# Layer 0's activation chain by one feature tile instead of two

## The chip, the cores and the metric

The kernel runs on one core of a Trainium2 chip. The metric is the device time of one execution in microseconds (us); lower is better. Beside it the profiler leaves a trace of one execution, from which all rows below are taken.

## The reference

Three results are computed in one launch: an attention with a window of 128 and 4 sink tokens, and two dense layers one after the other on 1536 tokens. Cut to what matters here:

```
h = x @ w_in                                   # 1536x512 @ 512x2048
sp = np.where(h > 20.0, h, np.log1p(np.exp(np.minimum(h, 20.0))))
g = h * np.tanh(sp)                            # layer 0's activation
y = g @ w_out                                  # 1536x2048 @ 2048x512
...
g = h * np.clip(h + 3.0, 0.0, 6.0) / 6.0       # layer 1's, on y with its own weights
```

## The kernel before

**Work and stages.** Attention comes first, layer 0 next and layer 1 last, but they overlap. The attention of the first eight 128-token blocks is done alone; the remaining blocks' attention is cut into pieces that are issued from within layer 0's steps. All weights arrive as 64-bit words and are decoded on VectorE (DVE) and ScalarE (ACT): two mask and shift operations (L210, L211), one that joins them (L212), a float16 high part on ACT (L222) and the float16 rest on DVE (L224). Layer 1's weights take a check (L215 on ACT), their own splits (L249, L250) and some sums (L260 to L268). Every product is three float16 matmuls: high by high, high by low, low by high.

**A step of layer 0.** There are 24. A step has `up` (L728) and `down` (L766). `up` multiplies two feature tiles of 128 features by 512 tokens; each tile has 12 matmuls (L745 to L747) and its own PSUM bank `h`, out of the four of the pool `ps_h`. Then comes the activation chain: Exp out of PSUM (L748, ACT), Square (L753, ACT), Ln (L754, ACT), Exp (L755, ACT), the product with `h` (L757, DVE, which is the last reader of the bank), the float16 high half `gh` (L761, ACT) and the low half `gl` (L762, DVE). L748 and L757 go over one tile at a time, the other five over both tiles, 1024 elements per partition. `down` multiplies the result `g16` by the second weights (L790, 24 matmuls), adding to four banks of the pool `ps_acc`. It lags by one step, so TensorE (PE) sees up(s), down(s-1), up(s+1), down(s). Layer 1 has the same form (L814 to L832 up, L854 down, L875 the sums that free its accumulators).

**What shares the banks.** The attention's scores `s` (L349, L556; read by L353 and L563 on DVE) and its output `o` take banks of the same pool `ps_h` in turn.

**What sets the order.** `hook()` is called after each tile of `up` and twice in `down`. It issues the next pieces of attention and of the decode; the decode pieces have a lower priority. A scheduler then fixes for each engine one static queue, in which an instruction that waits holds up all behind it. Raw weights have two buffers, so a load starts when the decode two before is done.

Of the kernel before, what the change touches and what calls it, by code (L numbers as in the profile page):

```python
# [8 lines left out]
F16 = mybir.dt.float16  # L9
I32 = mybir.dt.int32  # L10
I16 = mybir.dt.int16
AF = mybir.ActivationFunctionType
ALU = mybir.AluOpType
# [8 lines left out]
SX = 12  # L22
SW = 12
SG = 12
# [5 lines left out]
def attention_moe_moe2(  # L30
# [13 lines left out]
    nc = tc.nc  # L44
# [21 lines left out]
    g_p = main.enter_context(tc.tile_pool(name="g", bufs=LAG + 1))  # L66
# [16 lines left out]
    one = const.tile([128, 1], F32)  # L83
    fifth = const.tile([128, 1], F32)
# [17 lines left out]
    def watch(ap):  # L102
        i = n_low[0]
        n_low[0] += 1
        sq = const.tile([128, 64], F32, tag="sq", name="sq")
        nc.vector.tensor_tensor_reduce(out=sq, in0=ap, in1=ap, scale=1.0, scalar=0.0, op0=ALU.mult, op1=ALU.max, accum_out=lows[:, i:i + 1])
# [620 lines left out]
    def per_bank(blk):  # L727
        return 512 // (len(blocks[blk]) * 128)  # L728

    def up(st):  # L730
        layer, blk, f = st
        T = len(blocks[blk]) * 128
        per = per_bank(blk)
        x = xt[blk]
        e = e_p.tile([128, 2, per * T], F32, tag="e", name="e")
        hps = []
        for i in range(2):
            hp = ps_h.tile([128, per * T], F32, tag="h", name="h")
            for m in range(per):
                w = wt[layer, 0, f + i * per + m]  # L740
                o = hp[:, m * T:(m + 1) * T]
                for c in range(KD):
                    wh = w[:, 0, c * 128:(c + 1) * 128]
                    wl = w[:, 1, c * 128:(c + 1) * 128]
                    nc.tensor.matmul(o, wh, x[:, 0, c, :], start=c == 0, stop=False)  # L745
                    nc.tensor.matmul(o, wh, x[:, 1, c, :], start=False, stop=False)  # L746
                    nc.tensor.matmul(o, wl, x[:, 0, c, :], start=False, stop=c == KD - 1)  # L747
            nc.scalar.activation(out=e[:, i], in_=hp, func=AF.Exp, scale=2.0 ** -(SW + SX))  # L748
            hps.append(hp)
            hook()  # L750


        nc.scalar.activation(out=e, in_=e, func=AF.Square, bias=one)  # L753
        nc.scalar.activation(out=e, in_=e, func=AF.Ln, bias=fifth, scale=0.2)  # L754
        nc.scalar.activation(out=e, in_=e, func=AF.Exp, scale=-1.0)  # L755
        for i in range(2):
            nc.vector.scalar_tensor_tensor(out=e[:, i], in0=e[:, i], scalar=2.5, in1=hps[i], op0=ALU.subtract, op1=ALU.mult)  # L757
        sc = -0.4 * 2.0 ** (SG - SW - SX)
        g16 = g_p.tile([128, 2, 2 * per, T], F16, tag="g16", name="g16")
        gh, gl = (g16[:, i].rearrange("p (a b) n -> p a (b n)", a=2) for i in range(2))  # L760
        nc.scalar.activation(out=gh, in_=e, func=AF.Copy, scale=sc)  # L761
        nc.vector.scalar_tensor_tensor(out=gl, in0=e, scalar=sc, in1=gh, op0=ALU.mult, op1=ALU.subtract)  # L762
        gt[st] = g16
        if blk == 0 and f == 0:
            watch(g16[:, 0, 0, 0:64])
# [180 lines left out]
    def hook():  # L946

        if "at1" in late:
            budget["credit"] += budget["att"] / 4
        while budget["credit"] >= 1:  # L950
            att_side.piece()
            budget["credit"] -= 1
        for _ in range(DPS):
            if dec_side.n < budget["lim"]:
                with tc.high_priority(offset=-DEC_BACK):
                    dec_side.piece()
        if budget["chk"]:
            chk_side.piece()
# [273 lines left out]
```

## Time and profile before

| what | value |
|---|---|
| median of 3 runs | 595.24 us (595.04 to 595.64) |
| the profiled execution | 595.09 us, of which the trace spans 593.3 us |
| PE busy | 576.4 us, 97% |
| DVE busy | 461.7 us, 78% |
| ACT busy | 401.3 us, 68% |

The profiled execution lies 0.15 us below the median, and 1.8 us of it lie outside the span. Busy shares are means over stages that differ much; the stage has to be looked at for each wait.

### The profile page before, as it was taken

Reading aid. Unit: us, or ns where it says so; the run is one execution under the profiler, and the core shown is the slowest. Engines: PE = TensorE matmul, PEld = TensorE weight load, DVE = VectorE, ACT = ScalarE, POOL = GpSimd, SP = SyncE. Lnnn points to the kernel's source line nnn. Section 1 sums busy time; section 2 is a strip of 40 time slices with the busy share of each in tenths; the row PEclk is TensorE's granted clock in tenths of the full one; section 3 lists DMA queues with packets and bytes.
Section 4 is the critical chain, followed back from the end, with each engine's and each line's share of the span. In section 5 each row is a group of like instructions: output and inputs, shape, how many; then the busy total and the mean of one; then the engine's idle time right before and its main releaser. Section 6 shows DMA issues by size and latency. Waiting matters only on the chain.

```text
span 593.3 us, 11399 instructions
## 1 busy us (share of the span) xinstructions
PE 576.4 (97%) x4426; PEld 393.8 (66%) x4426; DVE 461.7 (78%) x1106; ACT 401.3 (68%) x794; POOL 22.4 (4%) x40
## 2 busy tenths in 40 slices
PE   8999999999999999999999999999999999999996
PEld 4787754444545445544444468888888888888885
DVE  5789999599944347489998999976687889864754
ACT  5998787699787578678978886544354656553532
POOL 0141010400000000000000000000000000000000
PEclk9999999999999999999999999999999999999999
DMA  9976357999762122252545442200017676400001
GB/s 176 244 166 200 114 172 165 211 259 249 200 141 31 26 39 57 39 160 82 173 141 173 142 143 72 72 1 2 1 30 250 217 261 216 148 21 1 36 1 39
DMA packets 105842, 72.24 MB, mean 122 GB/s; under 512 B 73512, under 2 KB 98088, under 8 KB 105784
## 3 DMA queue, kind: packets, MB, share of 16 engines
q1 hardware_dynamic: 105784, 71.48, 43.7%
q8 instruction: 35, 0.57, 0.4%
q14 instruction: 23, 0.19, 0.1%
HBM read 60.43 MB, written 3.15 MB: 107 GB/s over the span
## 4 chain that ended last, share of the span: by engine, by line
PE 65%; DVE 18%; ACT 9%; issue 3%; DMA 3%; SPq 1%; POOL 0%; DVEq 0%; ACTq 0%; POOLq 0%
PE acc L854 17%; PE acc L790 10%; PE h L816 6%; PE h L814 6%; PE h L815 6%; PE h L745 4%; PE h L747 4%; PE h L746 3%; PE s L349 2%; PE o L390 2%; DVE p L212 2%; DVE e L757 2%; DVE w L268 2%; DVE g L762 2%; ACT e L753 1%
## 5 line engine op out<-in xcount | busy, mean ns | idle before, releaser
L790 PE MATMUL acc<-g,w 128*128 128x512 f16 x576 | 130.1, 379 | 2.1 <-DVE g L762 1.7
L854 PE MATMUL acc<-w,g 128*128 128x256 f16 x1008 | 114.0, 273 | 0.2 <-DVE ob L875 0.2
L854 PEld LDWEIGHTS <-g 128*128 128x128 f16 x1008 | 98.6, 98 | 11.8 <-issue 0.4
L815 PE MATMUL h<-xt,w 128*128 128x256 f16 x384 | 104.7, 273 | 0.0
L816 PE MATMUL h<-xt,w 128*128 128x256 f16 x384 | 104.7, 273 | 0.0
L814 PE MATMUL h<-xt,w 128*128 128x256 f16 x384 | 104.7, 273 | 0.0
L790 PEld LDWEIGHTS <-w 128*128 128x128 f16 x576 | 55.3, 98 | 68.2 <-issue 3.4
L745 PE MATMUL h<-xt,w 128*128 128x512 f16 x192 | 72.8, 379 | 3.8 <-DVE e L757 3.6
L747 PE MATMUL h<-xt,w 128*128 128x512 f16 x192 | 72.8, 379 | 0.0
L746 PE MATMUL h<-xt,w 128*128 128x512 f16 x192 | 72.8, 379 | 0.0
L818 ACT ACTIVATE e<-h,bias 128x512 f32<-128x512 f32 x48 | 32.5, 678 | 47.7 <-PE h L816 47.6
L819 DVE SCALAR_TENSOR_TENSOR e<-e,h 128x512 f32<-128x512 f32 x48 | 32.7, 682 | 38.0 <-ACT e L818 38.0
L831 ACT ACTIVATE g<-e 128x256 f16<-128x256 f32 x96 | 29.5, 354 | 30.1 <-DVE e L819 30.1
L831 ACT ACTIVATE g<-sm 128x512 f16<-128x512 f32 x48 | 30.2, 628 | 27.3 <-DVE sm L826 27.2
L757 DVE SCALAR_TENSOR_TENSOR e<-e,h 128x512 f32<-128x512 f32 x48 | 30.8, 683 | 19.6 <-ACT e L755 19.5
L748 ACT ACTIVATE e<-h 128x512 f32<-128x512 f32 x48 | 28.2, 588 | 18.6 <-PE h L747 18.6
L832 DVE SCALAR_TENSOR_TENSOR g<-sm,g 128x512 f16<-128x512 f32 x48 | 33.0, 687 | 10.0 <-ACT g L831 9.9
L815 PEld LDWEIGHTS <-w 128*128 128x128 f16 x384 | 37.6, 98 | 4.5
L814 PEld LDWEIGHTS <-w 128*128 128x128 f16 x384 | 37.6, 98 | 4.5
L816 PEld LDWEIGHTS <-w 128*128 128x128 f16 x384 | 37.6, 98 | 4.4
L212 DVE SCALAR_TENSOR_TENSOR p<-raw,y 128x1024 int32<-128x1024 int32 x32 | 39.4, 1232 | 0.4
L746 PEld LDWEIGHTS <-w 128*128 128x128 f16 x192 | 18.8, 98 | 24.6 <-issue 3.6
(176 smaller groups left out, 949.4 us busy)
## 6 DMA issues: line engine op xcount, KB each, us to landing
raw<-in_moe_w_in_dram SPq DMA_DIRECT2D x48, 512.0 KB, 4.1
raw<-in_moe_w_out_dram SPq DMA_DIRECT2D x48, 512.0 KB, 5.1
out_dram<-ob SPq DMA_DIRECT2D x12, 256.0 KB, 2.6
first<-in_k_dram SPq DMA_DIRECT2D x8, 256.0 KB, 4.6
first<-in_q_dram SPq DMA_DIRECT2D x8, 256.0 KB, 5.0
first<-in_v_dram SPq DMA_DIRECT2D x8, 256.0 KB, 4.7
nk<-in_k_dram SPq DMA_DIRECT2D x5, 256.0 KB, 3.2
nv<-in_v_dram SPq DMA_DIRECT2D x5, 256.0 KB, 3.1
```

The costliest lines, as they stand in the source:

```text
L212: nc.vector.scalar_tensor_tensor(out=p, in0=t[:, :, 1], scalar=3, in1=y, op0=ALU.logical_shift_left, op1=ALU.bitwise_xor)
L745: nc.tensor.matmul(o, wh, x[:, 0, c, :], start=c == 0, stop=False)
L746: nc.tensor.matmul(o, wh, x[:, 1, c, :], start=False, stop=False)
L747: nc.tensor.matmul(o, wl, x[:, 0, c, :], start=False, stop=c == KD - 1)
L757: nc.vector.scalar_tensor_tensor(out=e[:, i], in0=e[:, i], scalar=2.5, in1=hps[i], op0=ALU.subtract, op1=ALU.mult)
L790: nc.tensor.matmul(o, l_, r_, start=first and m == 0 and x == 0, stop=last and end and x == 2, skip_group_check=True)
L814: nc.tensor.matmul(o, wh, x[:, 0, c, :], start=c == 0, stop=False)
L815: nc.tensor.matmul(o, wh, x[:, 1, c, :], start=False, stop=False)
L816: nc.tensor.matmul(o, wl, x[:, 0, c, :], start=False, stop=c == KD - 1)
L831: nc.scalar.activation(out=g[:, 0, d_], in_=src, func=AF.Copy, scale=sc)
L832: nc.vector.scalar_tensor_tensor(out=g[:, 1, d_], in0=src, scalar=sc, in1=g[:, 0, d_], op0=ALU.mult, op1=ALU.subtract)
L854: nc.tensor.matmul(a[n // 2][:, n % 2], l_, r_, start=f == fa and m == 0 and n % 2 == 0 and x == 0, stop=ends and m == 1 and x == 2 and (n ...
```

## The change

After a tile's matmuls, all seven operations of its chain are issued for that tile alone, each on 512 elements per partition, and then `hook()` is called. Before, `hook()` stood right behind the first Exp of a tile, and the rest of the chain behind both tiles. The tile `g16` is now allocated at the start of `up`, and its layout in memory is unchanged. In the changed file the chain stands at L749 to L756: first Exp L749, Square L750, Ln L751, second Exp L752, product L753, `gh` L755, `gl` L756; later lines are five less than before (L790 is L785, L875 is L870).

```
-        hps = []
+        g16 = g_p.tile([128, 2, 2 * per, T], F16, tag="g16", name="g16")
+        sc = -0.4 * 2.0 ** (SG - SW - SX)
         for i in range(2):
...
             nc.scalar.activation(out=e[:, i], in_=hp, func=AF.Exp, scale=2.0 ** -(SW + SX))
-            hps.append(hp)
+            nc.scalar.activation(out=e[:, i], in_=e[:, i], func=AF.Square, bias=one)
+            nc.scalar.activation(out=e[:, i], in_=e[:, i], func=AF.Ln, bias=fifth, scale=0.2)
+            nc.scalar.activation(out=e[:, i], in_=e[:, i], func=AF.Exp, scale=-1.0)
+            nc.vector.scalar_tensor_tensor(out=e[:, i], in0=e[:, i], scalar=2.5, in1=hp, op0=ALU.subtract, op1=ALU.mult)
+            gh, gl = (g16[:, x, i * per:(i + 1) * per].rearrange("p a n -> p (a n)") for x in range(2))
+            nc.scalar.activation(out=gh, in_=e[:, i], func=AF.Copy, scale=sc)
+            nc.vector.scalar_tensor_tensor(out=gl, in0=e[:, i], scalar=sc, in1=gh, op0=ALU.mult, op1=ALU.subtract)
             hook()
-
-
-        nc.scalar.activation(out=e, in_=e, func=AF.Square, bias=one)
-        nc.scalar.activation(out=e, in_=e, func=AF.Ln, bias=fifth, scale=0.2)
-        nc.scalar.activation(out=e, in_=e, func=AF.Exp, scale=-1.0)
-        for i in range(2):
-            nc.vector.scalar_tensor_tensor(out=e[:, i], in0=e[:, i], scalar=2.5, in1=hps[i], op0=ALU.subtract, op1=ALU.mult)
...
-        nc.scalar.activation(out=gh, in_=e, func=AF.Copy, scale=sc)
-        nc.vector.scalar_tensor_tensor(out=gl, in0=e, scalar=sc, in1=gh, op0=ALU.mult, op1=ALU.subtract)
```

**First place: DVE, third step of layer 0 and the one after it, near 115 us of the trace.** In the rows a name is followed by its number; `e` and `h` of one step carry the same `e`. Before, the chain of the third step (e_1416), the loads' splits of the next attention block, and the decode of raw_1560 ahead of the fourth step's two products (e_1527):

```order
L757 SCALAR_TENSOR_TENSOR e_1416<-e_1416,h_1447 128x512
L516 SCALAR_TENSOR_TENSOR v16_1523<-nv_1493,v16_1523 128x512
L762 SCALAR_TENSOR_TENSOR g16_1474<-e_1416,g16_1474 128x1024
L534 SCALAR_TENSOR_TENSOR q16_1727<-nq_1549,q16_1727 128x512
L508 SCALAR_TENSOR_TENSOR k16_1697<-nk_1551,k16_1697 128x512
...
L210 TENSOR_SCALAR y_1810<-raw_1560 128x1024
L211 TENSOR_SCALAR y_1810<-raw_1560 128x1024
L757 SCALAR_TENSOR_TENSOR e_1527<-e_1527,h_1528 128x512
L757 SCALAR_TENSOR_TENSOR e_1527<-e_1527,h_1565 128x512
```

After the change, the same place; e_1542 is the fourth step, and raw_1521 is the weight tile that comes before the one decoded there earlier (as raw_1506 it stood, before the change, ahead of the third step's L757):

```order
L508 SCALAR_TENSOR_TENSOR k16_1730<-nk_1573,k16_1730 128x512
L753 SCALAR_TENSOR_TENSOR e_1542<-e_1542,h_1544 128x512
...
L516 SCALAR_TENSOR_TENSOR v16_1749<-nv_1575,v16_1749 128x512
L756 SCALAR_TENSOR_TENSOR g16_1543<-e_1542,g16_1543 128x512
L210 TENSOR_SCALAR y_1697<-raw_1521 128x1024
L211 TENSOR_SCALAR y_1697<-raw_1521 128x1024
L212 SCALAR_TENSOR_TENSOR p_1698<-raw_1521,y_1697 128x1024
L753 SCALAR_TENSOR_TENSOR e_1542<-e_1542,h_1587 128x512
L210 TENSOR_SCALAR y_1842<-raw_1582 128x1024
L224 SCALAR_TENSOR_TENSOR w_1705<-p_1698,w_1705 128x2x512
```

The first tile's product moved ahead of the decode, and three decode operations moved in between the two products of the step; the decode as a whole stands one weight tile further back.

**Second place: DVE, the fifth step.** Before, the decode of raw_1675, and then both products of the step (e_1649) side by side:

```order
L210 TENSOR_SCALAR y_1939<-raw_1675 128x1024
L211 TENSOR_SCALAR y_1939<-raw_1675 128x1024
L212 SCALAR_TENSOR_TENSOR p_1940<-raw_1675,y_1939 128x1024
L757 SCALAR_TENSOR_TENSOR e_1649<-e_1649,h_1650 128x512
L757 SCALAR_TENSOR_TENSOR e_1649<-e_1649,h_1680 128x512
```

After the change, with e_1669 for the same step:

```order
L753 SCALAR_TENSOR_TENSOR e_1669<-e_1669,h_1671 128x512
L210 TENSOR_SCALAR y_1976<-raw_1702 128x1024
L211 TENSOR_SCALAR y_1976<-raw_1702 128x1024
L224 SCALAR_TENSOR_TENSOR w_1850<-p_1843,w_1850 128x2x512
L756 SCALAR_TENSOR_TENSOR g16_1670<-e_1669,g16_1670 128x512
L212 SCALAR_TENSOR_TENSOR p_1977<-raw_1702,y_1976 128x1024
L753 SCALAR_TENSOR_TENSOR e_1669<-e_1669,h_1707 128x512
```

Five operations now stand between the products of the two tiles, four of them decode.

**Third place: DVE at the end of layer 1's first group of accumulators, near 380 us.** L875 frees the accumulators, L268 is decode. Before:

```order
L875 SCALAR_TENSOR_TENSOR ob_4291<-acc_4103,ob_4290 128x256
L832 SCALAR_TENSOR_TENSOR g7_4241<-sm_4171,g7_4241 128x512
L875 SCALAR_TENSOR_TENSOR ob_4290<-acc_4104,ob_4291 128x256
L268 SCALAR_TENSOR_TENSOR w_4162<-t_4157,w_4162 128x4x256
L268 SCALAR_TENSOR_TENSOR w_4163<-p_4057,w_4163 128x256
L268 SCALAR_TENSOR_TENSOR w_4163<-p_4129,w_4163 128x2x256
L875 SCALAR_TENSOR_TENSOR ob_4291<-acc_4104,ob_4291 128x256
```

After the change (L870 is the former L875, L827 the former L832):

```order
L268 SCALAR_TENSOR_TENSOR w_4283<-p_4249,w_4283 128x2x256
L827 SCALAR_TENSOR_TENSOR g7_4361<-sm_4291,g7_4361 128x512
L870 SCALAR_TENSOR_TENSOR ob_4411<-acc_4223,ob_4410 128x256
L870 SCALAR_TENSOR_TENSOR ob_4410<-acc_4224,ob_4411 128x256
L870 SCALAR_TENSOR_TENSOR ob_4410<-acc_4226,ob_4410 128x256
```

The first two of the seven releases moved from ahead of the last decode operations to behind them.

## Rows read from the trace of the kernel before

**Rows 1.** The page: busy time, share of the span and instructions by engine

```profile
PE 576.4 (97%) x4426; PEld 393.8 (66%) x4426; DVE 461.7 (78%) x1106; ACT 401.3 (68%) x794; POOL 22.4 (4%) x40
```

**Rows 2.** Waits of PE: line, waited for, total us, times, longest us

```profile
PE h L745 <- DVE e L757: 3.6, 2, 2.4
PE acc L790 <- DVE g L762: 1.7, 2, 1.1
```

**Rows 3.** Timeline of PE at those waits, and at the last: start, duration, line, idle before

```profile
119.86 0.38 PE L745 MATMUL h<-xt,w 128*128 128x512 f16 x1 [2.38 <-DVE e L757]
...
144.60 0.38 PE L745 MATMUL h<-xt,w 128*128 128x512 f16 x1 [1.26 <-DVE e L757]
...
319.50 5.12 PE L790 MATMUL acc<-g,w 128*128 128x512 f16 x23 [0.66 <-DVE g L762]
...
331.09 2.10 PE L790 MATMUL acc<-g,w 128*128 128x512 f16 x9 [1.07 <-DVE g L762]
...
382.78 1.47 PE L854 MATMUL acc<-w,g 128*128 128x256 f16 x12 [0.24 <-DVE ob L875]
```

**Rows 4.** Busy time by stretch: PE, PEld, DVE, ACT, POOL, clock, DMA share, GB/s

```profile
117.50:157.10 39.60, 35.80 (x246) 17.34 (x247) 38.64 (x67) 35.74 (x63) 0.68 (x1) 1.00 1.00 241
...
160.00:250.80 90.80, 90.80 (x644) 44.04 (x643) 46.48 (x100) 66.83 (x110) 0.00 (x0) 1.00 0.30 60
...
350.00:382.60 32.60, 32.54 (x275) 26.71 (x274) 32.58 (x81) 20.26 (x42) 0.00 (x0) 1.00 0.24 82
```

**Rows 5.** ACT by line: form and count, busy us, mean ns, idle before

```profile
L753 ACT ACTIVATE e<-e,one 128x1024 f32<-128x1024 f32 x24 | 27.5, 1146 | 0.6
L761 ACT ACTIVATE g<-e 128x1024 f16<-128x1024 f32 x24 | 25.3, 1054 | 11.4 <-DVE e L757 11.3
```

**Rows 6.** DVE by line, same columns

```profile
L757 DVE SCALAR_TENSOR_TENSOR e<-e,h 128x512 f32<-128x512 f32 x48 | 30.8, 683 | 19.6 <-ACT e L755 19.5
L762 DVE SCALAR_TENSOR_TENSOR g<-e,g 128x1024 f16<-128x1024 f32 x24 | 29.4, 1225 | 7.1 <-ACT g L761 7.1
L832 DVE SCALAR_TENSOR_TENSOR g<-sm,g 128x512 f16<-128x512 f32 x48 | 33.0, 687 | 10.0 <-ACT g L831 9.9
```

**Rows 7.** Timeline of ACT, one step of layer 0

```profile
294.71 0.62 ACT L267 ACTIVATE w<-p 128x512 f16<-128x512 f32 x1
295.23 1.04 ACT L761 ACTIVATE g<-e 128x1024 f16<-128x1024 f32 x1
296.17 0.58 ACT L748 ACTIVATE e<-h 128x512 f32<-128x512 f32 x1
...
298.57 1.15 ACT L753 ACTIVATE e<-e,one 128x1024 f32<-128x1024 f32 x1
299.76 1.15 ACT L754 ACTIVATE e<-e,fifth 128x1024 f32<-128x1024 f32 x1
300.94 1.06 ACT L755 ACTIVATE e<-e 128x1024 f32<-128x1024 f32 x1
```

**Rows 8.** Timeline of DVE around 114 to 124 us

```profile
114.45 0.69 DVE L508 SCALAR_TENSOR_TENSOR k<-nk,k 128x512 f16<-128x512 f32 x1 [1.88 <-ACT k L507]
...
117.67 0.75 DVE L210 TENSOR_SCALAR y<-raw 128x1024 int16<-128x1024 int16 x1 [1.81 <-DMA raw<-in_moe_w_out_dram]
118.30 0.74 DVE L211 TENSOR_SCALAR y<-raw 128x1024 int16<-128x1024 int16 x1
119.11 1.28 DVE L757 SCALAR_TENSOR_TENSOR e<-e,h 128x512 f32<-128x512 f32 x2
...
122.78 1.22 DVE L212 SCALAR_TENSOR_TENSOR p<-raw,y 128x1024 int32<-128x1024 int32 x1
123.91 0.69 DVE L508 SCALAR_TENSOR_TENSOR k<-nk,k 128x512 f16<-128x512 f32 x1
```

**Rows 9.** Waits of DVE from 250 to 383 us

```profile
DVE y L210 <- ACT e L753: 1.3, 1, 1.3
DVE g L762 <- ACT g L761: 1.2, 1, 1.2
```

More of the change, by code (lines that the diff above doesn't have):

```diff
@@ L748, in up @@
             nc.scalar.activation(out=e[:, i], in_=hp, func=AF.Exp, scale=2.0 ** -(SW + SX))
-            hps.append(hp)
-            hook()
-        nc.scalar.activation(out=e, in_=e, func=AF.Square, bias=one)
-        nc.scalar.activation(out=e, in_=e, func=AF.Ln, bias=fifth, scale=0.2)
-        nc.scalar.activation(out=e, in_=e, func=AF.Exp, scale=-1.0)
-        for i in range(2):
-            nc.vector.scalar_tensor_tensor(out=e[:, i], in0=e[:, i], scalar=2.5, in1=hps[i], op0=ALU.subtract, op1=ALU.mult)
-        sc = -0.4 * 2.0 ** (SG - SW - SX)
-        g16 = g_p.tile([128, 2, 2 * per, T], F16, tag="g16", name="g16")
-        gh, gl = (g16[:, i].rearrange("p (a b) n -> p a (b n)", a=2) for i in range(2))
-        nc.scalar.activation(out=gh, in_=e, func=AF.Copy, scale=sc)
-        nc.vector.scalar_tensor_tensor(out=gl, in0=e, scalar=sc, in1=gh, op0=ALU.mult, op1=ALU.subtract)
+            nc.scalar.activation(out=e[:, i], in_=e[:, i], func=AF.Square, bias=one)
[5 more added lines that the diff above has]
+            nc.vector.scalar_tensor_tensor(out=gl, in0=e[:, i], scalar=sc, in1=gh, op0=ALU.mult, op1=ALU.subtract)
+            hook()
         gt[st] = g16
```

## The prediction

> **What bounds the kernel now.** The page comes first: PE is busy 97% of the span, DVE 78%, ACT 68% [rows 1]. Busy matmuls are not the same as useful ones, but they say that no other engine holds PE up for long. The waits of PE come second, because the change removes no matmul: it can gain only what PE waits for a tile of layer 0's chain. There are two such entries, the bank of `h` that L757 frees, 3.6 us in 2 waits, and `g` from L762, 1.7 us in 2 waits [rows 2]. The timeline of PE puts them at 119.86 and 144.60 (2.38 and 1.26 us) and at 319.50 and 331.09 (0.66 and 1.07) [rows 3]. So the whole chain, made free, would be worth 3.64 + 1.73 = 5.37 us, and 5.61 with the 0.24 at 382.78. Third comes what the engines do in those stretches. From 117.5 to 157.1 DVE is busy 38.64 of 39.60 us and ACT 35.74; from 350 to 382.6 DVE is busy 32.58 of 32.60; from 160 to 250.8 PE never pauses and DVE is idle half the time [rows 4]. A wait of PE in the two full stretches is thus a matter of how much DVE has to do ahead of L757 or L762, and only partly of how long the chain is.
>
> **What the change costs.** Four ACT operations of 24 steps go from one of 1024 to two of 512: 96 more instructions. Standing alone, a 512 takes 0.62 us and a 1024 1.04 to 1.05 [rows 5, 7], so a split costs 2 x 0.62 - 1.05 = 0.19 us. In a full queue only starts count: 295.23 - 294.71 = 0.52 for 512, 296.17 - 295.23 = 0.94 for 1024 [rows 7], so 0.10 us each. That is 0.4 us per step of some 10.4, 9.6 us in all (18 at the upper end), on an engine that is idle 192 us; in the full stretch ACT has 3.86 us of idle time for some 4 x 0.4 = 1.6. I count it at nothing, hidden under PE. If that cover is gone, it is 1.6 us there. On DVE L762 becomes 24 more instructions. A 512 of this form takes 0.687 against 1.225 for 1024 [rows 6]: 0.15 us each when it stands alone, 3.6 us in all. In a full queue two products that stand together show 1.28 us from start to end [rows 8], so the second starts 0.60 after the first; a 1024 (L212, 122.78 to 123.91) starts its successor after 1.13, and 2 x 0.60 - 1.13 = 0.07 us each, 1.7 in all. Where DVE is full the queue price holds.
>
> [...]
>
> **What it gains.** From the end of a tile's matmuls a chain now needs 0.60 (first Exp), 1.19 (298.57 to 299.76), 1.18 and 1.09 for the three operations on 1024 [rows 7], then 1.30 for two L757 and 1.09 and 1.25 for L761 and L762: the banks are free after 5.4 us, `g` is there after 7.7. With 512 it is 0.60, then two operations with a pointer (0.62 + 1.146 - 1.054 = 0.71, and 0.04 between), 0.65, 0.72, 0.66 and 0.70: bank free after 3.5, `g` after 4.8. The first tile's chain also starts 2.6 us earlier (12 matmuls at 0.216, from starts such as those of the 23 from 319.50). This is a gain of latency, not of work.
>
> **The first stretch, 117 to 157 us.** The 2.38 at 119.86 goes: before, the product stood behind L210, which waited for its weights until 117.67 [rows 8]; now the first tile's product stands ahead of the decode, as the first place of the order shows. But the second tile's product stands behind L210, L211 and L212. Walked through with these durations: L508 ends near 115.1, the first product runs at about 115.7, PE starts its tile near 117.2 and wants the second bank at 119.8; `gl` ends at about 118.0, then 0.63 + 0.81 + 1.13 of decode bring the second product to 120.6, and it ends at 121.2. PE waits 1.4. One step on, the second place of the order, four decode operations and one `gl` stand between the products (0.63 + 0.64 + 1.13 + 0.60 + 1.13 = 4.1 us), and a pair of attention scores, which takes the bank of the second tile, waits about 2.2 us. So 3.6 us of new waits take the place of 3.64: I put the term at zero. The bounds: at best the second tile's product is in time, and 3.64 is gained. At worst the decode that was moved back counts. The weight tile in question was decoded before 114.45, when DVE had time (it idled 1.88 and 1.81 us there [rows 8]); now its 0.63 + 0.64 + 1.13 + 1.13 = 3.5 us fall into a stretch with 0.96 us to spare: 2.5 us lost, 2.8 with four split L762.
>
> **160 to 250 us.** PE is dense and DVE half idle [rows 4]: nothing is gained here, and a late DVE catches up. Whatever PE is ahead or behind at 157 stays until the end, unless DVE stops it after 250.
>
> **250 to 383 us.** Decode of layer 1 makes DVE full again. Its own waits for the chain are 1.3 (L753) and 1.2 (L761) [rows 9]; both shrink, DVE runs 1 to 2 us ahead of before, and `g` comes 2.9 us sooner: the 0.66 and 1.07 go, 1.73 gained. Part is given back. Between 350 and 382.6 DVE has nothing idle, so there PE can't stay further ahead than DVE does. DVE's lead is at most 2.5, less some 10 splits at 0.07 = 0.7, less new waits in the ping-pong of L210 with ACT's L215; I take 0.5. And all seven releases of the accumulators now stand behind the last decode, the third place. So the wait at 382.78 is not 0.24 but about 1.0 to 1.2, and of 1.73 some 0.75 remain. Bounds: 1.97 (also the 0.24 goes), and a loss of about 1.0 if DVE has no lead at all there. After that PE is dense, nothing is late.
>
> **Sum.** 595.09 + 0 - 0.75 = 594.3 for the profiled execution; with the 0.15 that it lies below the median, 594.5 us. That is within 0.2% (1.2 us), about what a measurement of this kernel can tell from no change.
>
> **Rivals.**
> - *All waits go* (faster): second tiles' products in time in the first stretch as well. For it: the second chain is ready 3 us sooner than before, and the scheduler may have left DVE enough between. Against it: the two order places. All of 5.6 gives 589.6; half of the first stretch and 1.2 of the second give 592.2. Chance of faster than 0.2%: 0.36.
> - *DVE's moved decode decides* (slower): the second tile's bank comes later by more than the time that PE spends on the first tile. It decides from 2.6 us between the products plus what was late before; I found 3.2 to 4.1 us, so some wait is certain and only its size is open. Price: 2.8 in the first stretch, carried to the end, less 0.75: 597.3; with the 1.0 lost at 383, 599. Against it: DVE had both waits to give back. Chance 0.18.
> - *The fixed cost per instruction decides* (slower): chains of 512 cost 1.6 us more ACT in the first stretch, 1.7 us more DVE, and ACT holds L570, L583 and L222 back behind them. In full, 595.24 + 3.3 = 598.5. Against it: ACT's idle time there is 3.86, and DVE's splits outside the full stretches are hidden. Chance 0.06. [...]
> - *No net effect* (the forecast): new waits take the place of old. Chance 0.40, with an own range of 594.05 to 596.4.
>
> **Range.** From 592.2 (half of the gains) to 597.3 (the moved decode) about 2 in 10 stay out: some 0.12 below, 0.08 above. Faster by over 0.2%: 0.36; within: 0.40; slower: 0.24.
>
> **What would show it.** Right: no wait of 2.4 us of PE for the product near 119, but one or two of 1 to 2.5 us between 119 and 135 for the second tile's product (L753 then); no waits for `g` at 319 and 331; a wait for L870 near 382 of about 1 us; ACT busy some 10 us more, DVE 2 to 4. Wrong on the fast side: PE's waits for L753 sum up to less than 2 us. Wrong on the slow side: waits above 5 us between 117 and 160, or DVE late at 250. The forecast rests most on the durations walked through at 115 to 135: a load that lands 1 us later or earlier moves all of it.

## The result, and the profile after the change

The change makes the kernel slower: 599.94 us median (598.12 to 600.91, 5 runs) against 595.24 (594.76 to 596.03, 5 runs), a ratio of 1.0071 with an interval of 1.0055 to 1.0087. The forecast was 594.5, in a range of 592.2 to 597.3. The execution profiled below took 600.69 us, its span is 598.8, so 5.5 us more than the span before.

The page's first part, to be set beside [rows 1]: PE's share is the same 97%, but PE is busy 3.6 us longer, with the same 4426 matmuls.

```profile
PE 580.0 (97%) x4426; PEld 395.4 (66%) x4426; DVE 465.3 (78%) x1130; ACT 414.2 (69%) x890; POOL 23.0 (4%) x40
```

The waits of PE (line, waited for, us, times, longest), beside [rows 2]. The two entries of before are gone; two waits of attention scores for the second tile's product stand there, one for the accumulators, and a smaller one for the tile's bank (0.86, in the timeline below).

```profile
PE s L556 <- DVE e L753: 3.7, 2, 2.0
PE acc L849 <- DVE ob L870: 2.8, 1, 2.8
```

The timeline of PE at these waits, beside [rows 3]; the lines from 171.47 to 174.78 are matmuls behind the wait near 170.

```profile
121.10 0.38 PE L746 MATMUL h<-xt,w 128*128 128x512 f16 x1 [0.86 <-DVE e L753]
...
134.23 0.87 PE L556 MATMUL s<-kt,qt 64*128 64x128 f16 x12 [1.98 <-DVE e L753]
...
169.84 0.51 PE L556 MATMUL s<-kt,qt 64*128 64x128 f16 x11 [1.70 <-DVE e L753]
...
171.47 0.63 PE L747 MATMUL h<-xt,w 128*128 128x512 f16 x1
171.89 0.63 PE L748 MATMUL h<-xt,w 128*128 128x512 f16 x1
...
174.57 0.38 PE L746 MATMUL h<-xt,w 128*128 128x512 f16 x1
174.78 0.38 PE L747 MATMUL h<-xt,w 128*128 128x512 f16 x1
...
386.08 6.29 PE L849 MATMUL acc<-w,g 128*128 128x256 f16 x42 [2.81 <-DVE ob L870]
```

From 171.5 to 174 the starts are 0.43 us apart, later 0.21: the matmuls go at half speed. The 42 at 386.08 take until 392.21, when the next matmul starts, where their count and the spacing elsewhere (0.109) make 4.6. The view by stretch says the same of the granted clock (columns as in [rows 4]):

```profile
169.80:176.00 6.20, 6.16 (x30) 2.59 (x30) 3.82 (x13) 5.17 (x13) 0.00 (x0) 0.72 0.62 87
...
386.10:389.00 2.90, 2.90 (x14) 2.06 (x15) 2.83 (x8) 0.13 (x1) 0.00 (x0) 0.50 0.00 0
```

A clock of 0.50 is half of the 1.00 that stands in all of [rows 4]; the mean of 0.72 holds a stretch of each (0.50 from 171.4 to 174.0, 0.99 from 174.2 to 176.0). By these means, 0.28 of 6.2 us and 0.26 of the 6.1 from 386.1 to 392.2 (clock 0.74), that is about 3.3 of the 3.6 us that PE is busy longer.

Where the 5.5 us arise is seen best by setting the start of the same matmul in both timelines side by side (us; a step's first L745 before, L746 after; in layer 1 a step's first L814 and L809):

```
first matmul of                       before    after    behind
first step of layer 0                  71.90    72.28    +0.38
eighth step                           156.80   156.89    +0.09
ninth step, first tile                168.28   170.28    +2.00
ninth step, second tile               170.88   174.57    +3.69
seventeenth step                      261.22   264.91    +3.69
last step of layer 0                  336.05   337.43    +1.38
layer 1, fourth step                  376.48   377.87    +1.39
layer 1, fifth step                   386.71   392.21    +5.50
```

So nothing is lost up to 157 us; 3.6 us are lost between 157 and 175; 2.3 are won back from 261 to 337; 4.1 are lost near 383. After that both run alike. These are the places of one execution: e1 and e8 below run the same instructions in the same order on PE, DVE and ACT up to 330 us, by their traces, and at the seventeenth step PE is 4.03 behind in the one and 1.90 in the other.

### The profile page after: what moved, and what is told of

Read it like the earlier page. It is cut to its first block, busy times and chain, and to the rows that moved or that the text cites. A ratio compares the mean times of both kernels' runs of the same rounds, so it can differ in the third digit from the quotient of the medians.

```text
span 598.8 us, 11492 instructions
## 1 busy us (share of the span) xinstructions
PE 580.0 (97%) x4426; PEld 395.4 (66%) x4426; DVE 465.3 (78%) x1130; ACT 414.2 (69%) x890; POOL 23.0 (4%) x40
## 4 chain that ended last, share of the span: by engine, by line
PE 69%; DVE 15%; ACT 10%; DMA 2%; issue 2%; SPq 1%; POOL 0%; DVEq 0%; ACTq 0%; POOLq 0%
PE acc L849 17%; PE acc L785 11%; PE h L810 6%; PE h L811 6%; PE h L809 6%; PE h L746 4%; PE h L747 4%; PE h L748 4%; PE o L390 2%; PE s L349 2%; DVE p L212 2%; PE tp L368 2%; DVE w L268 1%; DVE g L756 1%; DVE y L210 1%
## 5 line engine op out<-in xcount | busy, mean ns | idle before, releaser
L785 PE MATMUL acc<-g,w 128*128 128x512 f16 x576 | 129.5, 379 | 0.0
L849 PE MATMUL acc<-w,g 128*128 128x256 f16 x1008 | 115.4, 275 | 2.8 <-DVE ob L870 2.8
L809 PE MATMUL h<-xt,w 128*128 128x256 f16 x384 | 104.7, 273 | 0.0
L785 PEld LDWEIGHTS <-w 128*128 128x128 f16 x576 | 55.4, 98 | 65.4 <-issue 0.2
L746 PE MATMUL h<-xt,w 128*128 128x512 f16 x192 | 73.6, 383 | 0.9 <-DVE e L753 0.9
L814 DVE SCALAR_TENSOR_TENSOR e<-e,h 128x512 f32<-128x512 f32 x48 | 32.7, 681 | 38.2 <-ACT e L813 38.2
L753 DVE SCALAR_TENSOR_TENSOR e<-e,h 128x512 f32<-128x512 f32 x48 | 32.7, 682 | 21.5 <-ACT e L752 21.5
L827 DVE SCALAR_TENSOR_TENSOR g<-sm,g 128x512 f16<-128x512 f32 x48 | 32.9, 686 | 10.5 <-ACT g L826 10.4
L756 DVE SCALAR_TENSOR_TENSOR g<-e,g 128x512 f16<-128x512 f32 x48 | 33.1, 689 | 10.2 <-ACT g L755 10.2
L810 PEld LDWEIGHTS <-w 128*128 128x128 f16 x384 | 37.6, 98 | 4.6
L809 PEld LDWEIGHTS <-w 128*128 128x128 f16 x384 | 37.6, 98 | 4.5
L811 PEld LDWEIGHTS <-w 128*128 128x128 f16 x384 | 37.6, 98 | 4.4
L212 DVE SCALAR_TENSOR_TENSOR p<-raw,y 128x1024 int32<-128x1024 int32 x32 | 39.3, 1229 | 0.4
L750 ACT ACTIVATE e<-e,one 128x512 f32<-128x512 f32 x48 | 34.4, 717 | 0.9
```

Source lines behind the costliest of these rows:

```text
L212: nc.vector.scalar_tensor_tensor(out=p, in0=t[:, :, 1], scalar=3, in1=y, op0=ALU.logical_shift_left, op1=ALU.bitwise_xor)
L750: nc.scalar.activation(out=e[:, i], in_=e[:, i], func=AF.Square, bias=one)
L756: nc.vector.scalar_tensor_tensor(out=gl, in0=e[:, i], scalar=sc, in1=gh, op0=ALU.mult, op1=ALU.subtract)
L785: nc.tensor.matmul(o, l_, r_, start=first and m == 0 and x == 0, stop=last and end and x == 2, skip_group_check=True)
L849: nc.tensor.matmul(a[n // 2][:, n % 2], l_, r_, start=f == fa and m == 0 and n % 2 == 0 and x == 0, stop=ends and m == 1 and x == 2 and (n ...
```

## The experiments

Two theories stood at the start. A: the loss sits at the two places where a release on DVE stands behind decode work, and the clock of PE falls in the waits there. B: the 120 added instructions make ACT and DVE late by their own time. C, D and E are named in the expectations where they come in. For each run PE is compared with before in the same way as above; the numbers are collected behind the last experiment.

**e1: the releases of the accumulators ahead of the last decode.**

```
+        with tc.high_priority(offset=60):
             nc.scalar.activation(out=A[:, 0], in_=p[0], func=AF.Copy, scale=sc)
             add(B[:, 0], p[5], A[:, 0])
...
```

> The changed kernel, with one thing undone: the eight operations that end a group of layer 1's accumulators (the seven L870 and the copy before them) get a higher priority, so that on DVE they stand ahead of the last decode operations again, as before the change. Nothing upstream of that place moves. Theory A (the loss sits at two places where a release stands behind decode work, near 170 us and near 386 us, and after each of these waits the clock of TensorE is low for some microseconds): the wait of 2.81 us near 386 falls to 0.5 us or less, the stretch of low clock behind it (1.5 us) goes too, and the time is about 599.9 - 4.0 = 595.9 us (595.0 to 597.0). Theory B (96 more instructions on ACT and 24 more on DVE make these engines late everywhere): the wait comes back at the next place where PE needs DVE, and the time stays within 1 us of 599.9. Theory C (the low clock is not tied to the waits): the wait goes but a stretch of low clock stays, 597.4.

Measured: 597.45 us (596.11 to 599.27, 10 runs), 1.0026 [1.0013, 1.004]. The timeline of PE near 386:

```profile
385.40 2.13 PE L849 MATMUL acc<-w,g 128*128 128x256 f16 x18 [0.60 <-DVE ob L870]
...
387.80 0.39 PE L849 MATMUL acc<-w,g 128*128 128x256 f16 x2 [0.26 <-ACT g L826]
...
388.88 1.38 PE L849 MATMUL acc<-w,g 128*128 128x256 f16 x11 [0.69 <-DVE g L827]
```

The long wait and the low clock are gone (the granted clock is 1.00 from 383 to 392), which is 2.5 us of the median; less than the 4 expected, since three short waits remain, 1.55 us together: one for a release, and two for `g` of layer 1, which stands later now. So DVE itself is late there, and its order decides only in part.

**e2: the decode one step sooner.** `DECS = [5, 7, 9, 10, 11, ...]` in place of `[5, 7, 8, 9, 10, ...]`.

> The changed kernel, with the limit of layer 0's weight decode raised by one weight tile from the third step on, so that the last tile's decode (L210, L211, L212, L222, L224) is issued a step sooner; on ACT the last L222 then stands ahead of the ninth step's first Exp instead of between its Square and its Ln. Theory A: the wait of 1.70 us near 170 us and the low clock after it (together 3.6 us) go, unless the decode that is sooner costs as much between 117 and 157 us, where DVE is full; 596.3 us if it costs nothing there, up to 599 if it does. Theory B: the wait stays or moves by a step, 599.5 to 600.5. In both the wait near 386 stays at 2.5 to 3 us.

(The step called the ninth in the expectations of e2, e4 and e9 is the eighth: the wait near 170 stands ahead of the ninth, for a product of the eighth.)

Measured: 598.95 us (597.91 to 599.3, 5 runs), 1.0054 [1.0036, 1.0071]. The wait near 170 fell to 0.91 without a low clock (1.00 from 168 to 174), another grew to 1.76 near 145; the 2.81 near 384 stayed. So moving the decode moves the waits, but by itself it tells little apart.

**e3 and e4: each half of the edit alone.** e3 is the kernel before with both calls of `hook()` behind the chain; e4 is the changed kernel with `hook()` behind the first Exp again.

> The kernel before, with one half of the change: both calls of hook() stand behind the chain instead of behind the first Exp of each tile; the chain still goes over both tiles. Theories A and B: the split matters and not the place of hook(): 595.2 us, give or take 1. Theory D (hook() being later makes decode and attention late): 597.5 or more, with waits near 170 and 386 like those of the changed kernel.

> The changed kernel, with the other half undone: hook() stands behind the first Exp of a tile again, the chain goes over one tile at a time. Theory A: the seven L870 still stand behind the last decode operations and L222 still stands inside the ninth step's chain, so both waits stay, 598.5 to 600.5. Theory B the same. Theory D: both waits go, 595 give or take 1.

Measured: e3 595.98 us (594.8 to 597.58, 10 runs), 1.0007 [0.9996, 1.0018], no difference; e4 599.43 us (598.9 to 600.02, 4 runs), 1.0061 [1.0041, 1.0082], slower like the changed kernel. So the split is what costs, and D falls. The later `hook()` isn't without effect, though: in e3's profiled execution (596.65 us) the last L222 also waits for DVE, until 163.40 instead of 161.33, PE waits 0.84 near 169, and it is 1.39 behind at the seventeenth step.

**e5 and e6: the split in one part of the steps.**

```
+        if blk == 2:          # e6: if blk < 2
             ... (one tile at a time)
+        else:
             ... (both tiles, as before)
```

> The chain goes over one tile at a time in the third token block alone (the last eight of layer 0's 24 steps, after some 255 us), over both tiles as before in the first sixteen. Theory A, as the first four runs leave it: DVE's work from the seventeenth step to 382 us fills it without a gap, so its end follows the start of that stretch, and what PE gains there is given back at the accumulators' release. So: like before until 255 us; no waits near 319 and 331, TensorE 1.7 to 2.3 us ahead at 345 us; a wait for L870 near 382 of 2 to 2.5 us; at 400 us between 0.5 us ahead and equal, plus some 1.5 us if the clock falls after that wait. Time 595.0 to 597.0. Theory B (the added instructions make DVE late by their own time): behind by 1 us or more at 400 us beside any low clock, 596.5 to 598.5.

> The reverse: one tile at a time in the first sixteen steps, both tiles in the last eight. Theory A: the waits of 117 to 157 us like the changed kernel's, a wait of 1.7 us near 170 and up to 1.7 us of low clock after it, so 3 to 3.7 us behind at 250 us; then the waits near 319 and 331 as before, and 0.2 to 0.5 near 385: nothing regained and nothing given back, no low clock there. Time 597.0 (no low clock near 170) to 599.0. Theory E (the loss near 386 us comes from the first blocks): a wait above 2 us near 386 here too.

Measured: e5 598.35 us (597.71 to 600.49, 4 runs), 1.0046 [1.0029, 1.0063]; e6 597.23 us (596.0 to 600.62, 9 runs), 1.004 [1.002, 1.006]. Each half loses by itself, and the two losses add up to that of the whole within their intervals. e6 shows no wait above 0.2 near 386, so E falls. Its wait near 170 is there as expected, 1.96, but the clock fell behind another one, near 134 (0.72 over 6 us; behind the wait near 170 it is 1.00). e5 missed theory A's time. In the profiled execution 2.9 us were lost near 145, in a wait of 2.56 and a low clock (0.72 over the 6 us behind the wait), with the same instructions as before in that part; but the other three executions, at 597.7 to 598.4, are outside 595 to 597 too. In the third block PE won 2.1 us, and then gave back these and 2.4 more, at the release and in a low clock behind it (0.77 over 6 us):

```profile
386.13 4.12 PE L879 MATMUL acc<-w,g 128*128 128x256 f16 x24 [2.82 <-DVE ob L900]
```

**e7: one step of 24 undone,** the eighth.

> The changed kernel with one step of 24 undone: the eighth step, whose second tile's product comes late at 169 us, goes over both tiles as before. Theory A (in that step ACT starts late, behind an L222 that waits for the decode, and two chains one behind the other then free the second bank later than one chain over both tiles): no wait of over 0.5 us between 160 and 175, TensorE within 0.7 us of before at 250 us; the wait near 382 stays at 2 to 2.8 us, since it takes back what is gained at 319 and 331; time 595.0 to 597.0. Rival (the lateness of DVE's decode itself delays the release, however the chain is cut): a wait above 1 us stays near 168, time 598.5 or more.

Measured: 599.35 us (598.3 to 600.01, 4 runs), 1.006 [1.0043, 1.0078]. The rival is right: the wait moved to the whole chain's products (L782 here) and did not shrink.

```profile
171.10 0.58 PE L747 MATMUL h<-xt,w 128*128 128x512 f16 x1 [2.00 <-DVE e L782]
```

ACT says why. The last L222 of layer 0 waits for the decode's L212, and the chain of that step stands behind it:

```profile
165.34 1.06 ACT L222 ACTIVATE w<-p 128x1024 f16<-128x1024 f32 x1 [4.36 <-DVE p L212]
```

The pair of products of the eighth step starts at 170.36 here, 5.02 us after the start of this L222, and PE waits for the first of the two. In e3, whole too, it is 163.40 and 168.43, 5.03. Before the change:

```profile
161.33 1.06 ACT L222 ACTIVATE w<-p 128x1024 f16<-128x1024 f32 x1 [1.14 <-DVE p L212]
...
166.36 1.29 DVE L757 SCALAR_TENSOR_TENSOR e<-e,h 128x512 f32<-128x512 f32 x2 [0.32 <-ACT e L755]
```

That is 5.03 as well. In the changed kernel, with two chains one behind the other, PE waits for the second product:

```profile
169.10 0.68 DVE L753 SCALAR_TENSOR_TENSOR e<-e,h 128x512 f32<-128x512 f32 x1
```

It starts 5.19 us after its L222 (163.91). For the product that PE waits for, how the chain is cut makes 0.16 us there. What counts is when DVE has L212 done, and in the changed kernel that is 2.6 us later than before.

**e8: matmuls in the wait.**

```
+        if f == fa and blk == (0, 1) and fa == 0:
+            fill = ps_h.tile([128, 512], F32, tag="h", name="fill")
+            for _ in range(14):
+                nc.tensor.matmul(fill, wt[1, 0, f][:, 0, 0:128], xt[0][:, 0, 0, 0:512], start=True, stop=True)
```

> The changed kernel with 14 more matmuls of 128x512, whose result nobody reads, ahead of the first matmul that waits for the accumulators near 383 us; at 0.216 us each they last 3.0 us, the length of that wait, so that TensorE is not idle in it. Theory A (the clock falls because TensorE stood still for 2.8 us): the 42 matmuls behind take 4.6 us instead of 6.3, and the time falls by about 1.5 us to 598.4. Theory C (the clock falls at that place for another reason): 599.9 or more, and the matmuls stay slow.

Measured: 598.85 us (597.91 to 602.51, 6 runs), 1.0071 [1.0046, 1.0097]; the time alone doesn't tell it from the changed kernel. The timeline does:

```profile
384.60 1.55 PE L853 MATMUL acc<-w,g 128*128 128x256 f16 x12
386.33 3.44 PE L853 MATMUL acc<-w,g 128*128 128x256 f16 x30 [0.18 <-DVE ob L874]
389.60 0.27 PE L809 MATMUL h<-xt,w 128*128 128x256 f16 x1
```

The 42 matmuls now last 5.0 us with a wait of 0.18 in them, against 6.1. Here the clock stays at 1.00 (384 to 396). That fits the theory, but e7 and e9 kept theirs too (1.00 over the 6 us behind it) behind a wait at the same place left empty, of 2.83 us in e9, so one profile doesn't prove it.

**e9, e10, e11: the causes undone.** e9 gives the decode of the eighth to tenth tiles a higher priority; e10 adds the edit of e1; e11 is e5 with the edit of e1.

```
-                with tc.high_priority(offset=-DEC_BACK):
+                with tc.high_priority(offset=60 if 14 <= dec_side.n < 20 else -DEC_BACK):
```

> The changed kernel, with a higher priority for the weight decode of the eighth to tenth tiles (pieces 14 to 19): on DVE the tenth tile's L210, L211 and L212 stand again ahead of the fourth step's products, at a time when DVE waits for loads, as before the change, and the last L222 stands ahead of the ninth step's first Exp. Theory A, as mended by the eight runs (in all of them the second tile's last product follows the start of the last L222 by 5.0 to 5.2 us, whole chain or split; so it is the decode's lateness on DVE that makes TensorE wait near 170): L222 starts at 161.5 or sooner, no wait above 0.4 us from 160 to 175, TensorE within 0.7 us of before at 250 us; the wait for L870 near 383 and the low clock behind it stay, so 596.8 to 598.3. Theory B (the split's added instructions): a wait of 1 us or more near 170 and 599 to 600.

> e9 and e1 together: the split chain with the decode of the eighth to tenth tiles ahead and with the releases of layer 1's accumulators ahead of the last decode operations. Theory A: nothing of the loss is left, and what the split gains at 319 and 331 us is given back to DVE by 390 us: 595.5 give or take 0.8, the same as before. Theory B: 597 or more. If the shorter chain is worth something by itself, 594.5 or less.

> e5 with the releases ahead: the chain split in the last eight steps alone, the eight operations that end a group of accumulators ahead of the last decode operations. Theory A (order of the releases, and the clock that falls in the long wait, are the whole loss of the third block): no single wait above 1.2 us from 380 to 392, no low clock there, 595.5 give or take 0.8 against 598.35 of e5. Theory B: 597.5 or more. Theory C (the clock falls there anyhow): 597.

Measured: e9 602.09 us (599.46 to 603.93, 4 runs), 1.0095 [1.0062, 1.0127]; e10 597.96 us (596.91 to 599.2, 7 runs), 1.0045 [1.0029, 1.0061]; e11 595.83 us (594.82 to 598.47, 12 runs), 1.0005 [0.9992, 1.0018].

e9 and e10 have no wait between 160 and 175, as expected, but both miss theory A's time: they pay elsewhere. The sooner decode sooner issues the next weight loads (in e10 one is issued at 98.39, where the load of the attention's next k stood before), that load of k goes out at 104.77 instead of 98.66 and its transpose at 112.20 instead of 104.91. PE waits for the transpose, a wait that stands in no other run. In e10:

```profile
116.75 0.53 PE L556 MATMUL s<-kt,qt 64*128 64x128 f16 x12 [4.07 <-DMA kt<-k]
```

So they don't settle the first blocks' share by their time. In e10 the last L222 starts at 161.24, as early as before the change, though PE is 2.3 us behind at that point: with its decode ahead, the split's own instructions don't make it late.

e11 settles the third block. In the execution profiled, PE is 2.06 us ahead of before at the last step of layer 0 and 0.05 ahead at layer 1's fifth step. The gain is all given back, in the same three short waits as e1, and the clock doesn't fall before the last microsecond of the span. It is the best version with a split, and equals the kernel before.

**e12: the decode held back, with the chain whole.**

```
+                with tc.high_priority(offset=-200 if 16 <= dec_side.n < 18 else -DEC_BACK):   # in the kernel before
```

> The kernel before, its chain over both tiles, with one thing of the changed kernel brought about by other means: the decode of the ninth weight tile (pieces 16 and 17) gets a lower priority, so that it stands behind the fourth step's products on DVE and all later decode stands further back. Theory A (the decode's lateness on DVE makes TensorE wait near 170, whatever the chain's cut): the last L222 starts at 163.3 us or later instead of 161.3, measured against TensorE's own place; the products follow 5.0 us behind its start; TensorE waits 0.8 to 2 us for them near 169, and is 1 to 3.5 us behind at 250 us, the more if the clock falls; the wait near 382 stays at 0.2 to 0.5. Time 596.2 to 598.5. Rival (the split itself is what makes TensorE wait there): no wait above 0.3 us from 160 to 175, 595.5 give or take 0.7.

Measured: 597.94 us (597.03 to 599.08, 5 runs), 1.0042 [1.0027, 1.0056], as much as e6, without any split. The place is not the one expected: PE waits 1.83 at 132.01 and 2.48 at 146.91 for the products (a clock of 0.72 behind the latter), and being 4 us behind by then has no wait near 170, though the pair of products stands 5.03 us behind L222 again (166.00, 171.03). Holding that decode back is thus enough for a loss of that size; where PE meets it is open to other things.

**PE against before, all runs** (us behind at the first matmul of the eighth step, the seventeenth, the last of layer 0, layer 1's fourth and fifth; negative is ahead):

```
run       8th    17th   last   L1 4th  L1 5th   5th less 17th
changed  +0.09  +3.69  +1.38  +1.39   +5.50    +1.81   (low clock near 386)
e2       +0.71  +1.83  -0.48  -0.33   +4.10    +2.27   (low clock near 386)
e4       +1.26  +2.72  +0.41  +0.68   +4.93    +2.21   (low clock near 386)
e5       +2.89  +2.90  +0.85  +1.43   +5.34    +2.44   (low clock near 386)
e7       +0.08  +4.24  +1.93  +1.92   +4.91    +0.67
e9       +6.50  +6.50  +4.19  +5.30   +8.33    +1.83
e8       +0.98  +1.90  -0.41  -0.14   +2.89    +0.99
e1       +0.11  +4.03  +1.72  +2.27   +3.93    -0.10   (releases ahead)
e10      +2.30  +2.31  +0.00  +0.17   +1.81    -0.50   (releases ahead)
e11      -0.21  -0.21  -2.06  -1.70   -0.05    +0.16   (releases ahead)
e3       -0.02  +1.39  +1.59  +1.59   +1.57    +0.18   (chain whole)
e6       +0.61  +2.78  +2.71  +2.79   +2.38    -0.40   (whole there)
e12      +3.99  +4.00  +4.01  +4.01   +4.01    +0.01   (chain whole)
```

The last column is the share of the third block. Wherever the chain is split there, PE wins 1.8 to 2.3 us by the last step of layer 0. With the releases ahead or the chain whole, what is left at layer 1's fifth step is what PE was behind at the seventeenth, within 0.5: whatever was won is given back. DVE's work there has a length of its own: from layer 1's first L260 to the last L268 it takes 127.5 us before the change (254.20 to 381.73), 127.8 in the changed kernel (257.22 to 385.00), 127.9 in e2 and 127.5 in e12. With the releases behind the decode another 0.7 to 1.8 us are lost (e7, e8, e9), and up to 2.4 where the clock falls too.

## Why the prediction was wrong

By its own stretches, in the profiled execution: 0 was put for 117 to 157 us and 0.3 was won, 0 for 160 to 250 and 3.6 was lost, a gain of 0.75 for 250 to 383 and 1.8 was lost. PE's start into layer 0, 0.38 later, is the rest.

**What bounds the kernel:** right in its parts. The two waits of [rows 2] were what the chain could give, and both went. What it left out is that a new wait can come where there was none.

**The cost of the split:** the size was right and it is not the cause. L750 on 512 took 0.717 us and L751 0.713, where 0.71 was estimated. ACT's busy time rose by 12.9 us and DVE's by 3.6, the latter the upper of the two prices given. In e11 the added instructions of the third block are all there, in e1 and e10 those of all steps, and the last column shows at most 0.16 us for the third block's, against the kernel before; whether they eat a part of what is won there is not shown.

**117 to 157 us at zero:** right. Waits of 0.86, 1.98 and 0.54 took the place of 2.38 and 1.26; PE was 0.09 us behind at the eighth step, 0.38 at the start of layer 0.

**160 to 250 us, "nothing is gained here, and a late DVE catches up":** this step failed first. The moved decode was seen and priced (2.5 to 2.8 us, in the rival to which 0.18 was given), but at the wrong place, and the late DVE was taken to be harmless after 157. It was not, because ACT's queue is static too: L222 stands in the chain of the eighth step's first tile, between Square and Ln, and waited 2.88 us for DVE's L212:

```profile
160.31 0.72 ACT L750 ACTIVATE e<-e,one 128x512 f32<-128x512 f32 x1
163.91 1.06 ACT L222 ACTIVATE w<-p 128x1024 f16<-128x1024 f32 x1 [2.88 <-DVE p L212]
164.87 0.71 ACT L751 ACTIVATE e<-e,fifth 128x512 f32<-128x512 f32 x1
```

The second tile's product came at 169.10 on DVE, where the pair had started at 166.36, and PE waited 1.70, then ran at the low clock: 3.6 us where nothing was put. That the decode's place alone is what makes L212 late is supported by e2, e10, e7 and e12 and not shown by a run that moves only it in the split kernel without other waits in its place; e9 and e10 met the loads, e2 a longer wait near 145. The size is that of this execution: in e8, the same program up to 330 us, the clock fell near 134 (0.72) and PE lost 0.92 from the eighth to the seventeenth step.

**250 to 383 us, "DVE's lead 0.5, the wait about 1.0 to 1.2":** the second failure. The gain was right (2.3 us won, 1.73 forecast). But DVE had no lead. Its full stretch starts with layer 1's decode, whose first L260 stands some 7 us ahead of PE's seventeenth step. It started 3.0 us late, while PE was 3.7 late; the last L268 ended 3.3 late. Nor did its waits shrink: from 250 us to the release those for ACT's `g` went from 1.2 us in one to 2.3 in four, those for L215 from 2.7 to 3.4. The first matmul of the 42 stood at 381.72 before, without a wait, and stands at 386.08. Its wait was 2.81, with all seven releases behind the last decode as the order had shown, and behind the next tile's product (L814 at 382.04) too:

```profile
385.52 2.72 DVE L870 SCALAR_TENSOR_TENSOR ob<-acc,ob 128x256 f32<-128x256 f32 x7
```

The bound given, a loss of 1.0 in all, holds for the order of the releases alone in e7 and e8 (0.67 and 0.99) and not in e9 (1.83); it had nothing for a DVE that is late from the start, which was the sign named for the slow side ("DVE late at 250").

**The clock:** not in the sum at all. It cost 1.7 us near 170 (the second tile of the ninth step is 1.69 further behind than the first) and 1.5 near 386 (6.1 against 4.6), 3.2 of 5.5 us in the profiled execution. The four runs in which it fell near 386 (to 0.72 to 0.77 over 6 us) have 1.8 to 2.4 in the last column; the three with the releases in the same place and no fall have 0.7 to 1.8.

**Rivals:** "all waits go" was wrong because PE's wait is DVE's or ACT's queue and not the chain's length. "The moved decode decides" had the right sign and, with 597.3 to 599, the nearest time to the result of all, for a reason that was half the matter: its place was the first stretch, and the clock, 3.2 us, was no part of it. "The fixed cost per instruction" came as near with 598.5, and had the wrong cause.

## What to carry to other kernels

Where a scheduler fixes static queues, ask of every instruction that lands inside a chain what it waits for: here a decode that was late on DVE stopped a chain on ACT (2.88 us of wait at L222). The shorter chain gave nothing here, because DVE was full up to the next join: the 2.06 us that e11 was ahead at the last step of layer 0 were 0.05 at layer 1's fifth step. A long wait at the join cost more than itself: 2.81 us, and 1.5 more for the low clock behind it. Of a stretch that is full, find what starts it, because here being late at its start was paid in full at its end (DVE 3.0 us late at the first L260, 3.3 at the last L268).

## What was not expected of the hardware

Behind some waits of PE the matmuls ran at half speed, at a granted clock of 0.50 instead of 1.00, for about 3 us in the changed kernel: starts 0.43 us apart instead of 0.216. It cost 1.7 us there near 170 and 1.5 near 386. In the fourteen profiles PE has 28 waits of 1.7 us or more between 60 and 420 us; the granted clock of the 6 us behind them is 0.55 to 0.77 in 15 and 1.00 in 13. Behind the four waits of 1.2 to 1.6 us it is 1.00, and between the first 7 us of the span and its last 5 there is no low clock anywhere else. So in these profiles a standstill of 1.7 us or more goes before each fall, but what decides between 2.38 us without one ([rows 3]) and 1.70 with one is open. The length of the wait doesn't: the same 1.98 us near 134 stand in the changed kernel, e1 and e7 with a clock of 1.00 behind them, in e6 and e8 with 0.72, and up to there the changed kernel and e8 are one program. It makes the price of a wait uncertain by as much as the wait itself (1.7 us behind the 1.70 near 170). That it accounts for executions of one kernel that differ by 2 to 4 us (598.12 to 600.91 for the changed kernel) was the author's estimate and is shown by no run here.
